# A gated feed-forward and attention kernel: seven-product blocks taken over 288 rows instead of 256

## The chip, the cores and the metric

The kernel runs on one core of one Trainium2 chip. A core has five engines that each run their own list of instructions in order and meet through semaphores: TensorE (PE, matrix products; its weight loads are listed as PEld), VectorE (DVE), ScalarE (ACT), GpSimd (POOL) and SyncE (SP), which here issues all DMA transfers. Matrix products accumulate into PSUM, which has eight banks of 128 partitions by 512 float32. The metric is the time of one execution in microseconds (us), lower is better; a run is compared with others of the same kernel by the median.

## The reference

Input `x` has 2048 positions of 576 values. Two branches work on it and a gate per position mixes them:

```python
g = sigmoid((x * gate_w).sum(-1))
a = A(x)                                   # 32-head attention in 4 segments of 512, with a memory, then @ wo
b = (silu(x @ w_gate) * (x @ w_up)) @ w_down   # 576 -> 4608 -> 576
out = g * a + (1 - g) * b
```

The change touches `x @ w_gate` and `x @ w_up`: 576 rows of the contraction, 4608 output columns each, 2048 positions. All of it is to float32 accuracy, which the kernel gets from a fast product format by splitting each operand into a high part and a low part (what the high part lost) and adding three products: high by high, high by low, low by high.

## The kernel before

The span has a first phase of some 220 us (projections q, k, v of the four segments, and the memory), a second phase to about 1710 us (feed-forward and attention interleaved), and an end (output projection).

**The unit.** The feed-forward is cut into two halves of positions (two segments of 512 each; half 0 is segments 2 and 3, half 1 is segments 0 and 1) and 36 column tiles of 128. A unit is one half and one tile `f`: it makes 128 gate columns and 128 up columns for two blocks of 512 positions. That is a 2 by 2 block product: gate and up stand for the two blocks on one side, the two segments for those on the other, and the contraction is halved. The kernel does it with seven block products instead of eight (a Strassen-Winograd scheme): sums and differences of the blocks are formed ahead, seven products are made, and their results are added up on the way through PSUM. The function `seven` (L934) makes one of them: two 128-row chunks, three terms (high/low) each, so six matmuls over 512 columns. The two halves of the contraction are rows 0 to 255 and 256 to 511. The last 64 rows don't take part: they are held twice in a 128-row operand, and `rest2` (L942) adds them to each of the four outputs with two matmuls, eight a unit.

**The order of a unit** is written out by hand (from L994): product 0 into bank `a`, ACT copies it to bank `xx` (L995); product 1 into bank `y`, ACT copies it to the row `p5` (L998); product 2 onto `a`, DVE adds `a` and `p5` into `y` (L1002); product 3 onto `xx`, copied to `sg0` (L1006); product 4 onto `a`, copied to `xx` (L1010); ACT applies Silu to `sg0` (L1012); product 5 onto `y`, Silu into `sg1` (L1015); the rest onto `a`, DVE adds it to `p5` (L1020); product 6 onto `xx`; DVE multiplies `sg0` by `xx` (L1024) and `sg1` by `p5` (L1025). Product 2 of the next unit goes onto `a` again and so needs the copy L995 of its product 0 to be done; that copy writes `xx`, which L1024 reads.

**Beats.** After each product, and once more after the rest on `a`, the unit calls `tick` (k = 0 to 7). A tick runs what is due at that beat: preparation of coming weights (`defer(o + 1, ...)` of a step with number `o` puts it at k = o of the unit, or at k = o - 8 of the next), splitting of results, groups of the down product (`down_group`, L788) and attention steps. In half 0 every third unit (f divisible by 3, position q = 0) carries sixteen down groups and the attention between its products and lasts some 37 us; the two units after it (q = 1 and q = 2) carry neither and last some 11 us. In half 1 attention goes into all units.

**Weights.** In half 0, `w_make(f)` (L221) makes the operands of the next unit: four sums on POOL (L230), seven high parts on ACT (L234), seven low parts on DVE (L237), and for the last 64 rows two high parts on ACT (L241) and two low parts on DVE (L244); SP stores all of them in DRAM (L247, L250). The raw tiles hold 640 rows' worth (512 and twice 64) and are loaded two units ahead (`w_load`, L202). In half 1 `w_fetch` (L600) loads the stored operands back. Between the halves, ten beats of down groups and attention only let the operands of the second pair of segments be formed (`x_second`, L903). At the end of the first phase the first half's operands of x are formed (`first_sum`, `first_split`), and those steps of unit 0's preparation that have numbers under 8 are worked off by the last eight `v_step` calls, up to three a call; what is left of them runs after the last.

Of the kernel before, what the change touches and what calls it, by code (L numbers as in the profile page):

```python
# [52 lines left out]
SLOT = (0, 3, 2, 1, 4, 6, 5)  # L53
KR = 6 * DH
# [7 lines left out]
def gated_mix(ctx, tc, xT, wf, wd, wv, wo, beta, cmask, ident, bmask, out):  # L62
# [13 lines left out]
    rc = dram.tile([FT, 2, P, 2 * P], F32, name="rc")  # L76
    xsd = dram.tile([2, P, L], F32, name="xsd")
# [63 lines left out]
    def xs_tile():  # L141
        return xo.tile([P, L], F32R, name="xs", bufs=2)

    def x_tiles(s):
        j = 5 * (s % 2)
        return [x_slot(j + kt // 2, kt % 2) for kt in range(4)], xs_tile()
# [52 lines left out]
    def raw_tile():  # L199
        return rp.tile([P, NT * P], F32, name="raw")  # L200

    def w_load(f, u):  # L202
        r = raw_tile().rearrange("p (k n) -> p k n", n=P)
        nc.sync.dma_start(r, wf[f][:, u])
        return r

# [6 lines left out]
    wraw_of, wops, wrem = {}, {}, {}  # L213
# [4 lines left out]
    def rem_tile():  # L218
        return wop.tile([P, 2, P], F32R, name="wr_", bufs=3)

    def w_make(f):  # L221
        g, u = wraw_of.pop(f)
        ops, rem = [None] * 7, [None] * 2
# [25 lines left out]
        def rem_keep(z):  # L249
            nc.sync.dma_start(rc[f, z], f32(rem[z]).rearrange("p a n -> p (a n)"))  # L250
# [16 lines left out]
    with ExitStack() as st:  # L267
        qst_ = ExitStack()
        qps = [pool(qst_, f"qp{i}", 1, side="right") for i in range(2)]
# [13 lines left out]
        raws = {}  # L283

# [213 lines left out]

        FSUM = {4: [(1, 0), (4, 0)], 5: [(2, 0), (1, 1)], 7: [(4, 1), (2, 1)]}
        FSPLIT = {6: [(1, 0), (4, 0)], 7: [(2, 0), (1, 1)], 8: [(4, 1), (2, 1)]}  # L500
        for s in range(NSEG):
            upd = upd_gen(s - 1) if s else None
            casts = []
            for n, (m, u) in enumerate(chains):
# [13 lines left out]
                if (s, n) == (1, 7):  # L518
                    mid.append(betas)
                if s == 3:  # L520
# [13 lines left out]
            if s == 3:  # L534
# [4 lines left out]
                for i in range(NST):  # L539
                    qst.append(kq.tile([P, 2, L], BF, name=f"qst{i}"))  # L540
                    if i < NST - 1:
                        kst.append(kq.tile([P, 2, L], BF, name=f"kst{i}"))
# [5 lines left out]
                wraw_of[0] = [w_load(0, u) for u in range(2)]  # L548
                start = w_make(0)
            for n in range(8):  # L550
# [5 lines left out]
                if s < 2 and n == 6:  # L556
                    late.append((xsd[s], f32(xs_of[s][1])))
# [20 lines left out]
        while start[0][0] < 8:  # L578
            start.pop(0)[1]()
        for z in range(2):  # L580
# [3 lines left out]
    with ExitStack() as st:  # L584
# [15 lines left out]
        def w_fetch(f):  # L600
            ops, rem = [None] * 7, [None] * 2
# [6 lines left out]
            def two(z):  # L608
                rem[z] = rem_tile()
                nc.sync.dma_start(f32(rem[z]).rearrange("p a n -> p (a n)"), rc[f, z])  # L610

            return [(j + 2 if f else FIRST[j], lambda j=j: one(j)) for j in range(7)] + [(4 + 6 * (f == 0) + 4 * z, lambda z=z: two(z)) for z in range(2)]
# [3 lines left out]
        kst.append(kp.tile([P, 2, L], BF, name=f"kst{NST - 1}", bufs=1))  # L616
        defer(8, lambda: nc.gpsimd.memset(kst[NST - 1], -1.0))
# [193 lines left out]
        def c_open():  # L811
# [6 lines left out]
            for n, (hf, kt) in zip((1, 2, 4, 5, 8, 9), ((0, 0), (0, 2), (0, 4), (1, 0), (1, 2), (1, 4))):  # L818
                wo_load(n, hf, slice(kt, min(kt + 2, NT)))
# [3 lines left out]
        def wo_load(n, hf, k):  # L823
# [309 lines left out]
```

## Time and profile before

| what | us |
|---|---|
| median of three runs (lowest, highest) | 1810.26 (1809.39, 1811.24) |
| the profiled execution, time | 1809.34 |
| the profiled execution, span from first to last instruction | 1807.6 |
| PE busy in the span | 1792.1 |
| DVE busy | 1287.7 |
| ACT busy | 960.2 |
| POOL busy | 796.3 |

The span lies 1.7 us under the execution's own time, and that time 0.9 us under the median. Matmuls are pipelined, so a matmul shown as 0.39 us long leaves room for the next one after 0.23 us. A row of the timeline gives the start and the duration in us, the engine, the line of the kernel, the operation, the tiles written and read, shapes and count; in brackets the idle time of the engine before it and what ended that. Consecutive instructions of one engine overlap by about 0.1 us in it, since the next enters while the last drains.

### The profile page before, as it was taken

The page shows a single profiled execution, that of the slowest core. Times are in us where ns is not written, and L with a number is a line of the kernel's source. Part 1 is how long each engine was busy: PE and PEld are TensorE (multiplying, and loading weights), DVE is VectorE, ACT ScalarE, POOL GpSimd, SP SyncE. Part 2 cuts the span into 40 slices and gives each one's busy share as a digit, 9 for nine tenths or more (in the row PEclk, how much of TensorE's full clock was granted, in tenths as well). Part 3 has the DMA queues.
Part 4 walks back from the last instruction along what each step waited for, and adds up shares of the span by engine and source line. Part 5 has one row for each costly group of instructions (what it writes and reads, how often), then busy time and mean ns, then how long its engine had stood idle before and what let it go on. Part 6 is the DMA issues. An engine that isn't in the chain of part 4 may idle for free.

```text
span 1807.6 us, 36471 instructions
## 1 busy us (share of the span) xinstructions
PE 1792.1 (99%) x12517; PEld 1539.4 (85%) x12517; DVE 1287.7 (71%) x3285; ACT 960.2 (53%) x1827; POOL 796.3 (44%) x991
## 2 busy tenths in 40 slices
PE   9999999999999999999989999999999999999999
PEld 7899888888888888888877887887887887888899
DVE  6455666777877787778777677777777777764455
ACT  7656575456655665566546455455455455354511
POOL 3323731344444444444445545555555545553121
PEclk9999999999999999999999999999999999999999
DMA  7444495556746664566467446355455455355544
GB/s 237 161 148 171 152 344 202 163 192 235 239 139 208 238 229 151 194 240 239 134 237 225 147 139 202 124 156 186 141 167 176 136 157 188 117 160 179 195 143 138
DMA packets 204936, 331.34 MB, mean 183 GB/s; under 512 B 38416, under 2 KB 95888, under 8 KB 204752
## 3 DMA queue, kind: packets, MB, share of 16 engines
q1 hardware_dynamic: 204752, 329.02, 54.8%
q8 instruction: 99, 1.62, 0.4%
q14 instruction: 85, 0.70, 0.1%
HBM read 194.33 MB, written 134.61 MB: 182 GB/s over the span
## 4 chain that ended last, share of the span: by engine, by line
PE 94%; DVE 3%; DMA 2%; issue 0%; ACT 0%; SPq 0%; POOL 0%; DVEq 0%; ACTq 0%
PE bank L938 37%; PE bank L798 24%; PE bank L134 12%; PE bank L944 7%; PE bank L674 4%; PE bank L632 4%; PE bank L703 2%; PE bank L705 1%; PE bank L369 1%; DVE xo L112 1%; PE bank L415 1%; DMA kst<-stk 1%; PE bank L857 0%; DMA raw<-in_xT_dram 0%; DVE scr L639 0%
## 5 line engine op out<-in xcount | busy, mean ns | idle before, releaser
L798 PE MATMUL bank<-dw,hh 128*128 128x320 f32 (+1 forms) x2304 | 484.4, 303 | 5.8 <-DVE ya L803 4.9
L768 POOL TENSOR_TENSOR p<-pe,p 128x512 f16<-128x512 f32 x320 | 379.9, 1187 | 175.6 <-DVE p L766 121.0
L798 PEld LDWEIGHTS bank<-dw,hh 128*128 128x128 f32 x2304 | 379.4, 189 | 25.7 <-DVE ya L803 6.4
L678 ACT ACTIVATE pe<-bank 128x512 f32<-128x512 f32 x320 | 190.5, 595 | 330.8 <-PE bank L674 292.7
L798 PE MATMUL bank<-dw,hl 128*128 128x320 f32 (+1 forms) x1152 | 340.2, 295 | 0.3 <-DVE hl L112 0.3
L686 POOL TENSOR_SCALAR_AFFINE_SELECT pe<-pe 128x256 f32<-128x256 f32 (+1 forms) x320 | 144.3, 451 | 325.9 <-ACT pe L678 299.7
L803 DVE TENSOR_TENSOR ya<-bank,ya 128x320 f32<-128x320 f32 x352 | 157.3, 452 | 155.8 <-PE bank L798 151.7
L639 DVE CUSTOM_DVE_ANT_0 scr<-bank,cm 128x512 bf16<-128x512 f32 (+3 forms) x512 | 247.6, 484 | 23.4 <-PE bank L632 15.4
L798 PEld LDWEIGHTS bank<-dw,hl 128*128 128x128 f32 x1152 | 217.6, 189 | 0.9 <-DVE hl L112 0.9
L766 DVE CAST p<-pe 128x512 f16<-128x512 f32 x320 | 155.9, 488 | 0.0
L674 PE MATMUL bank<-qst,kst 111*128 111x512 bf16 (+3 forms) x512 | 150.9, 303 | 0.0
L632 PE MATMUL bank<-kst,qst 108*128 108x512 bf16 (+3 forms) x512 | 126.0, 299 | 2.2 <-DMA kst<-stk 0.9
L882 DVE TENSOR_TENSOR hl<-row,hh 128x512 fp32r<-128x512 f32 x120 | 105.7, 881 | 13.1 <-ACT hh L881 13.1
L1006 ACT ACTIVATE row<-bank 128x512 f32<-128x512 f32 x72 | 43.1, 599 | 122.8 <-PE bank L944 122.7
L230 POOL TENSOR_TENSOR ws<-raw 128x256 f32<-128x256 f32 x72 | 63.5, 882 | 91.7 <-DMA raw<-in_wf_dram 73.5
L1020 DVE TENSOR_TENSOR row<-bank,row 128x512 f32<-128x512 f32 x72 | 49.6, 689 | 70.7 <-PE bank L944 70.7
L1024 DVE TENSOR_TENSOR row<-bank,row 128x512 f32<-128x512 f32 x72 | 49.8, 691 | 58.8 <-PE bank L944 50.4
L134 PE MATMUL bank<-xo,qhi 128*128 128x512 f32 x288 | 91.5, 398 | 0.1
L1010 ACT ACTIVATE bank<-bank 128x512 f32<-128x512 f32 x72 | 41.9, 582 | 82.1 <-PE bank L938 79.7
L325 POOL TENSOR_TENSOR q<-qr,q 128x512 bf16<-128x512 f32 x36 | 43.8, 1216 | 91.9 <-ACT q L324 82.6
L703 PEld LDWEIGHTS <-p 128*128 128x128 f16 x1280 | 69.2, 96 | 10.2 <-issue 6.6
L674 PEld LDWEIGHTS <-kst 111*128 111x128 bf16 x512 | 48.5, 98 | 34.3 <-issue 19.9
(2104 smaller groups left out, 4180.4 us busy)
## 6 DMA issues: line engine op xcount, KB each, us to landing
raw<-in_wf_dram SPq DMA_DIRECT2D x72, 320.0 KB
dc<-dw SPq DMA_DIRECT2D x36, 576.0 KB
dw<-dc SPq DMA_DIRECT2D x36, 576.0 KB
stk<-q SPq DMA_DIRECT2D x32, 384.0 KB
draw<-in_wd_dram SPq DMA_DIRECT2D x36, 288.0 KB
vd<-vps SPq DMA_DIRECT2D x8, 912.0 KB
v<-vd SPq DMA_DIRECT2D x16, 456.0 KB
qst<-stk SPq DMA_DIRECT2D x128, 54.0 KB
```

Of the source, the lines that this page charges most:

```text
L134: nc.tensor.matmul(t, st[n], mv[n], start=(n == 0), stop=(n == 13))
L632: nc.tensor.matmul(t[:, c:c + w], qs[:KR, pr, P * i:P * i + P], ks[:KR, pr, 0:w], start=True, stop=True)
L639: nc.vector.tensor_tensor_reduce(scr[:, :w], t[:, c:c + w], cm[:, L - w:L], 1.0, -3.0e38, OP.add, OP.max, m[:, k:k + 1])
L674: nc.tensor.matmul(t[:, c:c + w], ks[:KR + 3, pr, P * j:P * j + P], qs[:KR + 3, pr, P * j:L], start=True, stop=True)
L678: nc.scalar.activation(pe, t, AF.Exp, scale=SCALE)
L686: nc.gpsimd.affine_select(d, d, pattern=pat, compare_op=OP.is_ge, fill=0.0, base=0, channel_multiplier=-1)
L766: nc.vector.tensor_copy(p1, pe)
L768: nc.gpsimd.tensor_sub(p2, pe, p1)
L798: nc.tensor.matmul(t, p, q[:, cs], start=(n == 0), stop=(n == 3 * CH - 1))
L803: nc.vector.tensor_add(ya[:, i, cs], t, ya[:, i, cs])
L938: nc.tensor.matmul(t, w[:, p, z], x[z][:, q], start=first and n == 0, stop=last and n == 5, skip_group_check=True)
L944: nc.tensor.matmul(t, w[:, p], xs, start=False, stop=p == 1, skip_group_check=True)
```

## The change

The 576 rows are halved as a whole: each block product now goes over 288 rows. Of the last 64 rows the first 32 go with the first half and the other 32 with the second, so they take part in the sums and differences like all others. Their three terms (high by high, high by low, low by high) stand one below the other in one operand of 96 rows, so one more matmul a product covers them: seven matmuls in each of seven products, 49 a unit, where there were 42 and the eight of `rest2`.

- The host hands over two more inputs: the last rows of x and of the two weights, each repeated three times down the partitions.
- `w_make` forms four sums of 96 rows by 128 on POOL (`rem_total`, k = 3, 3, 4, 4), rounds all seven remainder operands at once on ACT (`rem_high`, 96 by 896, k = 5), makes the low part on DVE for rows 64 to 95 (`rem_low`, 32 by 896, k = 6) and stores them with one DMA of 336 KB (`rem_keep`, k = 7). The two ACT copies, two DVE subtractions and two stores of 128 KB for the old rest are gone.
- The raw weight tiles are loaded without the last rows (256 KB instead of 320 KB, twice a unit); `r_load` loads those into a single buffer (192 KB) at k = 7.
- In half 1 one load of 336 KB at k = 1 replaces two of 128 KB.
- The remainder operands of x, seven of 96 by 512, are formed in segments 1 and 2 of the first phase (`rest_load`, `rest_sum`, `rest_split`); those of the second half are stored and fetched back between the halves with seven loads of 192 KB in place of two of 256 KB.
- The DVE addition to `p5` moves from behind the rest on `a` to behind product 4. The two ticks around the removed rest now follow each other with nothing between.
- Two of the four attention buffers `qst` move to another pool, and the output weights are loaded in six pieces by columns.

```diff
-        def rem_high(z, r):
-            rem[z] = rem_tile()
-            nc.scalar.activation(rem[z][:, 0], r, AF.Copy)
-
-        def rem_low(z, r):
-            nc.vector.tensor_sub(rem[z][:, 1], r, f32(rem[z][:, 0]))
+        def rem_total(j):
+            r = rraw_of[f][:RB]
+            o, p, q, sub = {4: (5, 0, 1, True), 1: (1, 1, 3, False), 2: (4, 1, 0, True), 5: (6, 2, 4, True)}[j]
+            (nc.gpsimd.tensor_sub if sub else nc.gpsimd.tensor_add)(r[:, o], r[:, p], r[:, q])
+
+        def rem_high():
+            rem.append(rem_tile())
+            nc.scalar.activation(rem[0][:RB], rraw_of[f][:RB], AF.Copy)
+
+        def rem_low():
+            nc.vector.tensor_sub(rem[0][64:RB], rraw_of.pop(f)[64:RB], f32(rem[0][64:RB]))
...
-        for z, r in ((0, g[:, 4]), (1, u[:, 4])):
-            o = LEAD + 4 + 2 * z
-            todo += [(o, lambda z=z, r=r: rem_high(z, r)), (o + 1, lambda z=z, r=r: rem_low(z, r)),
-                     (o + 2, lambda z=z: rem_keep(z))]
+        todo += [(3 + n // 2, lambda j=j: rem_total(j)) for n, j in enumerate((4, 1, 2, 5))]
+        todo += [(5, rem_high), (6, rem_low), (7, rem_keep)]
...
+    def r_load(f):
+        rraw_of[f] = rp.tile([P, 7, P], F32, name="rr", bufs=1)
+        nc.sync.dma_start(rraw_of[f][:RB, 0:4], wfr[f])
...
+        RSTEP = {4: (0, 3, -1), 5: (5, -4, 1), 6: (-2, 4), 7: (2, -6), 8: (6,)}
...
+                if 1 <= s < 3:
+                    if n == 2:
+                        rest_load(2 - s)
+                    for j in RSTEP.get(n, ()):
+                        mid.append(lambda j=j: rest_split(2 - s, j) if j >= 0 else rest_sum(-j))
...
-            return [(j + 2 if f else FIRST[j], lambda j=j: one(j)) for j in range(7)] + [(4 + 6 * (f == 0) + 4 * z, lambda z=z: two(z)) for z in range(2)]
+            def rest():
+                rem.append(rem_tile())
+                nc.sync.dma_start(f32(rem[0][:RB]).rearrange("p j n -> p (j n)"), rc[f])
+
+            return [(j + 2 if f else FIRST[j], lambda j=j: one(j)) for j in range(7)] + [(1 if f else 10, rest)]
...
-        def seven(t, w, x, first, last):
+        def seven(t, j, first=True):
+            w, x = ops[j], XO[j]
             n = 0
             for z in range(2):
                 for p, q in ((0, 0), (0, 1), (1, 0)):
-                    nc.tensor.matmul(t, w[:, p, z], x[z][:, q], start=first and n == 0, stop=last and n == 5,
+                    nc.tensor.matmul(t, w[:, p, z], x[z][:, q], start=first and n == 0, stop=False,
                                      skip_group_check=True)
                     n += 1
+            nc.tensor.matmul(t, rem[:RB, RPOS[j]], XR[j][:RB], start=False, stop=True, skip_group_check=True)
 
-        def rest2(t, w, xs):
-            for p in range(2):
-                nc.tensor.matmul(t, w[:, p], xs, start=False, stop=p == 1, skip_group_check=True)
...
                 if half == 0 and f + 2 < FT:
+                    plan.append((7, lambda f=f: r_load(f + 2)))
...
-            seven(a, w[4], XO[4], False, True)
+            seven(a, 4, False)
             xx = x_tile()
             nc.scalar.activation(xx, a, AF.Copy)
+            nc.vector.tensor_add(p5, a, p5)
             tick()
             nc.scalar.activation(sg0, sg0, AF.Silu)
-            seven(y, w[5], XO[5], False, False)
-            rest2(y, wr[0], XS[1])
+            seven(y, 5, False)
             nc.scalar.activation(sg1, y, AF.Silu)
             if half or q == 0:
                 exp_table()
             tick()
-            rest2(a, wr[1], XS[1])
-            nc.vector.tensor_add(p5, a, p5)
             tick()
-            seven(xx, w[6], XO[6], False, False)
-            rest2(xx, wr[1], XS[0])
+            seven(xx, 6, False)
             nc.vector.tensor_mul(sg0, xx, sg0)
             nc.vector.tensor_mul(sg1, p5, sg1)
```

More of the change, by code (lines that the diff above doesn't have):

```diff
@@ L579, in gated_mix @@
             start.pop(0)[1]()
+        r_load(1)
         for z in range(2):
@@ L616, in gated_mix @@
         kst.append(kp.tile([P, 2, L], BF, name=f"kst{NST - 1}", bufs=1))
+        for i in range(2, NST):
+            qst.append(kp.tile([P, 2, L], BF, name=f"qst{i}", bufs=1))
         defer(8, lambda: nc.gpsimd.memset(kst[NST - 1], -1.0))
```

113 lines of the change are left out of this document (67 added, 46 removed).

## The prediction, made before the result was known

> **What bounds the kernel now.** I read the page first (busy times, chain of work that ended last), then the waits of PE, then the chain in order of time for the pitch of a matmul.
>
> ```profile
> span 1807.6 us, 36471 instructions
> ...
> PE 1792.1 (99%) x12517; PEld 1539.4 (85%) x12517; DVE 1287.7 (71%) x3285; ACT 960.2 (53%) x1827; POOL 796.3 (44%) x991
> ...
> PE 94%; DVE 3%; DMA 2%; issue 0%; ACT 0%; SPq 0%; POOL 0%; DVEq 0%; ACTq 0%
> PE bank L938 37%; PE bank L798 24%; PE bank L134 12%; PE bank L944 7%; PE bank L674 4%; PE bank L632 4%; PE bank L703 2%; PE bank L705 1%; PE bank L369 1%; DVE xo L112 1%; PE bank L415 1%; DMA kst<-stk 1%; PE bank L857 0%; DMA raw<-in_xT_dram 0%; DVE scr L639 0%
> ```
> ```profile
> PE bank L798 <- DVE ya L803: 4.9, 6, 1.7
> ```
> ```profile
> 227.92 2.72 PE bank L938 x12
> 230.64 0.91 PE bank L944 x4
> ```
>
> PE is busy for 99% of the span and carries 94% of the chain; its largest wait sums to 4.9 us. So PE's issue is the time, and whatever makes PE wait is added to it in full. Twelve matmuls of the products take 2.72 us and four of the rest 0.91: 0.227 us each. The profiled execution took 1809.34 us (span 1807.6), 0.9 under the median of 1810.26; I sum changes and add them to either.
>
> **Matmuls removed.** A unit goes from 42 + 8 = 50 to 49 matmuls, in 72 units: 72 x 0.227 = 16.3 us less on PE. The new ones have 96 rows. The trace has no such row count; nearest are 111 rows:
>
> ```profile
> L134 PE MATMUL bank<-xo,qhi 128*128 128x512 f32 x288 | 91.5, 398 | 0.1
> ...
> L674 PE MATMUL bank<-qst,kst 111*128 111x512 bf16 x128 | 50.0, 391 | 0.0
> ```
>
> 398 ns with 128 rows, 391 with 111: the rows cost nothing and save nothing, and I take 0.227 for the new ones too. Half of the 16.3, 8.2 us, falls in half 1, where the operands are only fetched (80 KB more a unit, on SP, off PE's path) and nothing else is added: I count it in full.
>
> **What half 0 adds, and where.** Only units q = 1 and q = 2 (and unit 0, which has no down groups yet) are tight, as the stretches of one group of three show; the third row is from the first phase.
>
> ```profile
> 467.86:479.38 11.52, 11.52 (x54) 9.52 (x52) 9.77 (x20) 8.88 (x18) 6.97 (x9) 1.00 0.59 191
> 479.38:490.71 11.33, 11.33 (x51) 9.38 (x50) 9.37 (x17) 8.58 (x22) 3.01 (x5) 1.00 1.02 372
> ...
> 50.00:100.00 50.00, 50.00 (x298) 44.87 (x297) 26.90 (x73) 32.65 (x66) 17.00 (x19) 1.00 0.43 146
> ```
>
> The columns after the length are PE, PEld, DVE, ACT, POOL, clock, DMA share, GB/s. By busy time there is room: DVE 9.4 of 11.3, ACT 8.6. But these engines work in order, so I follow the order at the end of unit q = 1 (start 467.86), with these prices for the two new operations, whose size of 896 elements a partition lies beside 870:
>
> ```profile
> L111 ACT ACTIVATE vw<-xo 128x870 fp32r<-128x870 f32 x1 | 0.9, 917 | 0.0
> ...
> L112 DVE TENSOR_TENSOR vw<-xo,vw 128x870 fp32r<-128x870 f32 x1 | 1.1, 1066 | 0.7 <-ACT vw L111 0.7
> ```
> ```profile
> 475.30 1.52 PE L938 MATMUL bank<-xo,wo__5755 128*128 128x512 f32 x6
> 476.66 0.61 PE L944 MATMUL bank<-xs,wr__5655 128*128 128x512 f32 x2
> 477.11 0.62 PE L944 MATMUL bank<-xs,wr__5772 128*128 128x512 f32 x2
> 477.56 1.52 PE L938 MATMUL bank<-xo,wo__5769 128*128 128x512 f32 x6
> ...
> 479.38 1.52 PE L938 MATMUL bank<-xo,wo__5810 128*128 128x512 f32 x6
> ...
> 482.10 1.52 PE L938 MATMUL bank<-xo,wo__5837 128*128 128x512 f32 x6
> ```
> ```profile
> 477.77 0.63 ACT L1012 ACTIVATE row<-row 128x512 f32<-128x512 f32 x1
> 478.31 0.58 ACT L1015 ACTIVATE row<-bank 128x512 f32<-128x512 f32 x1
> 478.79 0.41 ACT L234 ACTIVATE wo__5837<-ws 128x256 fp32r<-128x256 f32 x1
> 479.10 0.41 ACT L234 ACTIVATE wo__5846<-raw 128x256 fp32r<-128x256 f32 x1
> ...
> 480.94 0.58 ACT L995 ACTIVATE bank<-bank 128x512 f32<-128x512 f32 x1 [0.35 <-DVE row L1025]
> ```
> ```profile
> 479.65 0.69 DVE L1024 TENSOR_TENSOR row<-bank,row 128x512 f32<-128x512 f32 x1 [0.86 <-PE bank L944]
> 480.26 0.68 DVE L1025 TENSOR_TENSOR row<-row 128x512 f32<-128x512 f32 x1
> ```
> ```profile
>   ACT bank L995: 9.4, 17
> ```
>
> I take 0.95 us for `rem_high` and 1.10 for `rem_low`, by elements per partition; that the latter spans 32 partitions and not 128 might make it as short as a quarter, 0.27, which is the lower end used below.
>
> Take product 5's start, 475.30, as 0. Before: product 6 runs from 2.26 to 4.08; DVE multiplies at 4.35 (L1024) and 4.96 (L1025); the copy L995 starts when L1025 ends, at 5.64 (the last row: it waited for L1025 17 times), ends at 6.22, and product 2 of the next unit, which needs it, is due at 6.80. Slack 0.58.
>
> After: PE needs 4 products of 7 matmuls up to that product 2, so it is due at 28 x 0.227 = 6.35. ACT is unchanged up to the high part at 3.49 (478.79, k = 5), since the Silu table holds it up and not PE. Behind that high part, at 3.80, now stands `rem_high`, 0.95 long, to 4.75. `rem_low` is DVE's next at k = 6, right after, because the second tick has no PE work in front of it any more; it waits for `rem_high`, starts at 4.78 and lets DVE go on 1.02 later (1.10 less the 0.08 by which neighbours overlap), at 5.80. L1024 and L1025 are queued behind it: 5.80 and 6.41, end 7.09. L995 runs 7.09 to 7.67, and product 2 starts at 7.72, not 6.35: **PE waits 1.37 us**. Twelve q = 1 units do this: 16.4 us.
>
> At the end of q = 2 no table load stands ahead, and a split of `dw` stands between:
>
> ```profile
> 486.63 1.52 PE L938 MATMUL bank<-xo,wo__5885 128*128 128x512 f32 x6
> ...
> 488.64 0.60 ACT L1015 ACTIVATE row<-bank 128x512 f32<-128x512 f32 x1 [0.33 <-PE bank L944]
> ...
> 490.15 0.76 DVE L882 TENSOR_TENSOR dw<-draw,dw 128x576 fp32r<-128x576 f32 x1
> ```
>
> From product 5's start 486.63: Silu (L1015) 0.20 behind the eight matmuls (1.81) before, so at 1.79 after seven (1.59); high part 0.50 later at 2.29, `rem_high` 2.60 to 3.55, `rem_low` 3.58, DVE free at 4.60, `dw` to 5.30, L1024, L1025 to 6.59, L995 to 7.17, product 2 at 7.22 instead of 6.35: 0.87 us. Eleven q = 2 units make weights for a next one: 9.6 us. In q = 0 units with down groups three groups of 9 matmuls lie between k = 5 and k = 6: nothing.
>
> Unit 0 has no groups, and the reload of the exponential's table stands ahead of its high part:
>
> ```profile
> 232.13 0.58 ACT L1015 ACTIVATE row<-bank 128x512 f32<-128x512 f32 x1
> ...
> 234.13 0.40 ACT L234 ACTIVATE wo__2641<-ws 128x256 fp32r<-128x256 f32 x1
> ```
>
> 2.00 us from L1015 to it, not 0.48 as in q = 1: the wait is 1.37 + 1.52 = 2.9 us, once.
>
> **The start of unit 0.** Of its preparation 21 steps instead of 15 have numbers under 8, and 17 fit into the `v_step` calls. In order, `rem_high` falls to the seventh call and `rem_low` to the eighth, behind that call's DVE work:
>
> ```profile
> 220.74 1.63 PE L938 MATMUL bank<-xo,wo__2349 128*128 128x512 f32 x6
> ...
> 224.21 0.46 DVE L422 TENSOR_TENSOR q<-bank,dn 128x288 f32<-128x288 f32 x1
> ...
> 226.26 1.20 PE L938 MATMUL bank<-xo,wo__2434 128*128 128x512 f32 x4 [0.21 <-DVE wo__2434 L237]
> ```
>
> Product 0's seventh matmul, due at 220.74 + 1.36 = 222.10, now needs `rem_low`, which ends at 224.67 + 1.10 = 225.8: 3.7 us. Before, the 21st matmul came at 226.26 and not at 220.74 + 20 x 0.227 = 225.28, so 1.0 was lost there already. Net 2.7.
>
> **The rest, at nothing.** Phase one: seven copies of 0.6 us on ACT, seven DVE subtractions of 0.7, four POOL sums of 1.2 a segment, under PE's full 50 us where ACT has 32.65 and DVE 26.90; if a transpose's copy comes late behind two of them, 1 us a segment at most. Between the halves 832 KB more are loaded, 2.3 us at the 372 GB/s above if exposed; needed only after the down groups, and loaded behind what waits there now. DVE's earlier addition to `p5` runs where DVE waits for PE. POOL's four sums (each between nothing and the 0.73 of a 128x256 one) come 9 us ahead of need in q = 1. In q = 2 they need `r_load`, which stands on SP behind `rem_keep`, and so behind `rem_low`:
>
> ```profile
> 478.42 1.09 SPq L204 DMA_DIRECT2D raw<-in_wf_dram  x1
> ...
> 484.18 0.73 POOL L230 TENSOR_TENSOR ws<-raw 128x256 f32<-128x256 f32 x1 [4.51 <-DMA raw<-in_wf_dram]
> ```
>
> A load issued in that dense stretch (DMA share 1.02) is used 5.8 us later. `rem_low` of q = 1 ends at 5.9, the load goes out at 6.4, lands at 12.2, the sums are done by 14.1 (0.46 each); `rem_high` of q = 2 is due at 12.5 + 2.6 = 15.1. One us of slack; I take nothing, and a microsecond or two per group of three as the upper end.
>
> **Sum.** -16.3 + 16.4 + 9.6 + 2.9 + 2.7 = +15.3 us: 1824.6 for an execution like the profiled one, 1825.6 as a median.
>
> **The rivals.** *Hidden, faster (other side).* The remainder chain stays off PE's path, as the idle fifth of DVE and ACT suggests; only the start's 2.7 remains: 1810.26 - 16.3 + 2.7 = 1796.7. Place: L995 at the head of units q = 2 and q = 0. It decides if `rem_high` and `rem_low` together cost 0.6 us instead of 1.97, or if L1024 doesn't queue behind `rem_low`. The order of the code speaks against it. Chance 0.13.
>
> *The copy released one step earlier.* L995 needs only L1024's result; if it waits no longer for L1025, each of 24 waits is 0.61 shorter: 1825.6 - 14.6 = 1811.0, no change. Against it: the 17 waits above. 0.04.
>
> *POOL slows DVE.*
>
> ```profile
> L882 DVE TENSOR_TENSOR hl<-row,hh x120: 676/686/1424, 237.8 to 1717.3; 128x512 fp32r<-128x512 f32 x120
> ```
>
> One subtraction of two SBUF operands takes 0.68 or up to 1.42 us. If POOL's sums (late by a late `r_load`, or t4 and t5 of the same beats) lie over `rem_low`, it takes twice as long: 24 x 1.0 more, 1850. Against it: POOL is busy for 3.0 of 11.3 us in q = 2. 0.08. The Trainium skill says the same of the engines (GPSIMD Engine Reference, "Key points": the SBUF interfaces are shared, and GpSimd contends with DVE instructions of two SBUF inputs); the trace agrees with its 1.42 beside 0.68.
>
> *A removed matmul is worth its weight load too.*
>
> ```profile
> L798 PEld LDWEIGHTS bank<-dw,hh 128*128 128x128 f32 x2304 | 379.4, 189 | 25.7 <-DVE ya L803 6.4
> ```
>
> If loads did not lie under running matmuls, each removed pair were worth 0.227 and its load, 0.189 by a row of equal shape, 0.416 in all: 72 x 0.416 = 30.0, 13.7 more than I count, so 1811.9, no change. Twelve pairs in 2.72 us exclude it nearly: 0.01. The Trainium skill states it (TensorE: Matmul & The Clock Gate, "The mechanism": loads overlap running matmuls only where the row groups differ); the trace disagrees, with 0.227 for a pair in equal row groups.
>
> **How the numbers follow.** Forecast 0.74, rivals 0.13, 0.04, 0.08, 0.01. About 0.2% (3.6 us) is what a measurement of this kernel tells from no change. Faster: 0.13. Within: 0.05. Slower: 0.74 + 0.08 = 0.82. The likeliest case's own range is 1814 to 1837 (0.4 us either way on 24 waits, and the start). With `rem_low` at 0.27 each wait is 0.8 shorter (0.57, 0.07, 2.1, start 1.9): -16.3 + 6.8 + 0.8 + 2.1 + 1.9 = -4.7, or 1805.6. So the range is 1806 to 1846: it takes in that end, the two no-change cases and half of the slowed DVE, and leaves out the hidden case.
>
> **What would show it.** PE idle ahead of product 2 (the third product's first matmul) by some 1.4 us in each q = 2 unit and 0.9 in each q = 0 unit of half 0, put down to the ACT copy behind product 0; DVE idle on `rem_high` ahead of a 1.1 us subtraction; half 1 shorter by 8 us and half 0 longer by some 23, its start included; 3.7 us of wait at the seventh matmul of unit 0. If half 0 shows no such wait, the forecast is wrong in its main step; if the waits are there with other lengths, `rem_low` or L1025's release is mis-sized.

## The result, and the profile after

The changed kernel takes 1859.88 us (median of 4 runs, 1859.72 to 1862.87); the kernel before, beside it, 1810.75. The ratio is 1.0274, with a 95% interval of 1.0256 to 1.0292. The forecast was 1825.6 with a range of 1806 to 1846: the direction was right, the size was not, +49 us in place of +15.3. The profiled execution took 1862.87, the longest of the four; its profile lies about 3 us above the others, which is why the profiled spans below differ by 53.6 us and the medians by 49.1.

The page of the changed kernel, its busy times and its chain:

```profile
span 1861.2 us, 36473 instructions
...
PE 1805.4 (97%) x12445; PEld 1530.7 (82%) x12445; DVE 1318.9 (71%) x3263; ACT 981.1 (53%) x1805; POOL 891.0 (48%) x1143
...
PE 81%; DVE 6%; ACT 5%; DMA 3%; issue 3%; SPq 1%; POOL 0%; ACTq 0%; DVEq 0%; POOLq 0%
```

PE carried 94% of the chain before and carries 81% now; DVE and ACT have come in. The waits of PE, largest first (total, times, longest):

```profile
PE bank L983 <- DVE rh L251: 19.4, 14, 3.7
PE bank L839 <- DVE ya L844: 18.5, 15, 2.1
PE bank L673 <- ACT pe L719: 3.6, 10, 0.4
```

In the changed file L980 is a product's six matmuls, L983 its 96-row matmul, L248 `rem_high`, L251 `rem_low`, L839 the down groups' matmul, L844 DVE's addition behind it, L673 an attention matmul and L719 the attention's exponential. The sum of DVE's L844 stood at 4.9 before; the other two are new. One group of three units before (only its last row is new here) and after, then the two halves of each; the columns are those of the prediction's stretches:

```profile
550.79:588.07 37.28, 37.28 (x309) 33.12 (x308) 29.49 (x82) 17.55 (x35) 17.29 (x23) 1.00 0.50 167
...
220.74:941.28 720.54, 713.47 (x4655) 616.64 (x4654) 565.40 (x1361) 410.84 (x854) 298.64 (x369) 1.00 0.61 211
941.28:1807.64 866.36, 860.01 (x6583) 728.84 (x6581) 594.58 (x1622) 409.81 (x698) 407.33 (x516) 1.00 0.52 163
```
```profile
557.08:568.51 11.43, 11.43 (x52) 9.37 (x51) 9.41 (x18) 7.85 (x15) 9.41 (x13) 1.00 0.50 152
568.51:581.21 12.70, 11.56 (x50) 9.16 (x49) 8.96 (x15) 9.24 (x20) 6.45 (x9) 1.00 1.00 357
581.21:620.89 39.68, 37.98 (x308) 32.93 (x307) 32.06 (x82) 18.89 (x36) 19.01 (x26) 1.00 0.50 168
...
221.94:995.26 773.32, 729.76 (x4618) 613.89 (x4617) 594.47 (x1328) 426.47 (x819) 386.43 (x510) 0.99 0.61 204
995.26:1861.16 865.90, 856.59 (x6547) 722.98 (x6545) 585.61 (x1622) 409.10 (x698) 401.77 (x516) 1.00 0.54 166
```

All of the loss is in half 0: 720.5 to 773.3 us. Half 1, forecast 8.2 us shorter, is 0.5 shorter. In half 0 the q = 1 unit is level, the q = 2 unit is 1.4 us longer, and the long q = 0 unit, in which I had expected nothing but a wait at its head, is 2.4 us longer. Adding up the units' lengths (start to start of a unit's first matmul) tells where the 53.6 us of the profiled spans come from:

| part | before | after | difference | forecast |
|---|---|---|---|---|
| up to unit 0 | 220.74 | 221.94 | +1.2 | 0 |
| units 0 to 2 | 35.32 | 45.26 | +9.9 | +6.3 |
| q = 0, 11 units (3 to 33) | 403.97 | 431.29 | +27.3 | +7.1 |
| q = 1, 11 units (4 to 34) | 126.66 | 126.77 | +0.1 | -2.5 |
| q = 2, 10 units (5 to 32) | 113.33 | 126.60 | +13.3 | +11.4 |
| unit 35 and the break | 41.26 | 43.41 | +2.2 | +1.1 |
| half 1 | 866.36 | 865.89 | -0.5 | -8.2 |

The head of a q = 2 unit in the trace after, in order of time:

```profile
568.51 1.54 PE L980 MATMUL bank<-xo,wo__6748 128*128 128x512 f32 x6
...
569.08 0.94 ACT L248 ACTIVATE rh<-rr 96x896 fp32r<-96x896 f32 x1
...
570.05 1.08 DVE L251 TENSOR_TENSOR rh<-rr,rh 32x896 fp32r<-32x896 f32 x1 [2.09 <-ACT rh L248]
...
571.17 0.69 DVE L1059 TENSOR_TENSOR row<-bank,row 128x512 f32<-128x512 f32 x1
...
571.20 0.50 PE L983 MATMUL bank<-xr,rh 96*128 96x512 f32 x1 [1.14 <-DVE rh L251]
...
571.78 0.68 DVE L1060 TENSOR_TENSOR row<-row 128x512 f32<-128x512 f32 x1
571.96 0.58 ACT L1034 ACTIVATE bank<-bank 128x512 f32<-128x512 f32 x1 [0.75 <-DVE row L1059]
```

The two durations were forecast at 0.95 and 1.10 and are 0.94 and 1.08; `rem_low` indeed stands on DVE ahead of the multiplications of the unit before, and waits for ACT. But PE doesn't stop at product 2, for the copy. It stops at the seventh matmul of product 0, which reads `rem_low`'s own result. The copy itself (L1034) starts at 571.96, when the first of the two multiplications has ended (571.86), and doesn't wait for the second (572.46).

In the q = 0 unit the same instruction hits something else:

```profile
610.56 1.94 DVE L251 TENSOR_TENSOR rh<-rr,rh 32x896 fp32r<-32x896 f32 x1
612.53 0.49 DVE L844 TENSOR_TENSOR ya<-bank,ya 128x320 f32<-128x320 f32 x1
...
613.08 0.41 PE L839 MATMUL bank<-dw,hh 128*128 128x320 f32 x1 [1.34 <-DVE ya L844]
```

Here `rem_low` takes 1.94 us, beside attention work on POOL (all 25 that run while POOL is idle take 1.08; of the 11 beside POOL's work 10 take 1.93 to 1.94):

```profile
610.35 1.21 POOL L809 TENSOR_TENSOR p<-pe,p 128x512 f16<-128x512 f32 x1 [1.12 <-PE bank L715]
611.51 1.26 POOL L727 TENSOR_SCALAR_AFFINE_SELECT pe<-pe 128x256 f32<-128x256 f32 x1
```

The addition that empties the accumulator of a down group waits behind it, and the next down group has nowhere to write.

### The profile page after: what moved, and what is told of

Its sections match the earlier page's. It is cut to its first block, busy times and chain, and to the rows that moved or that the text cites. A ratio compares the mean times of both kernels' runs of the same rounds, so it can differ in the third digit from the quotient of the medians.

```text
span 1861.2 us, 36473 instructions
## 1 busy us (share of the span) xinstructions
PE 1805.4 (97%) x12445; PEld 1530.7 (82%) x12445; DVE 1318.9 (71%) x3263; ACT 981.1 (53%) x1805; POOL 891.0 (48%) x1143
## 4 chain that ended last, share of the span: by engine, by line
PE 81%; DVE 6%; ACT 5%; DMA 3%; issue 3%; SPq 1%; POOL 0%; ACTq 0%; DVEq 0%; POOLq 0%
PE bank L980 32%; PE bank L839 21%; PE bank L136 11%; PE bank L983 6%; PE bank L715 3%; PE bank L673 3%; DVE rh L251 2%; PE bank L744 2%; ACT rh L248 1%; PE bank L746 1%; ACT L1051 1%; SPq L781 1%; DVE xo L114 1%; DMA kst<-stk 1%; PE bank L379 1%
## 5 line engine op out<-in xcount | busy, mean ns | idle before, releaser
L839 PE MATMUL bank<-dw,hh 128*128 128x320 f32 (+1 forms) x2304 | 489.7, 305 | 21.2 <-DVE ya L844 18.5
L839 PEld LDWEIGHTS bank<-dw,hh 128*128 128x128 f32 x2304 | 379.5, 190 | 41.6 <-DVE ya L844 21.9
L719 ACT ACTIVATE pe<-bank 128x512 f32<-128x512 f32 x320 | 190.0, 594 | 320.1 <-PE bank L715 297.6
L839 PE MATMUL bank<-dw,hl 128*128 128x320 f32 (+1 forms) x1152 | 341.1, 296 | 0.3 <-DVE hl L114 0.3
L844 DVE TENSOR_TENSOR ya<-bank,ya 128x320 f32<-128x320 f32 x352 | 157.6, 454 | 116.1 <-PE bank L839 111.5
L983 PE MATMUL bank<-xr,rh 96*128 96x512 f32 x504 | 202.8, 402 | 19.4 <-DVE rh L251 19.4
L839 PEld LDWEIGHTS bank<-dw,hl 128*128 128x128 f32 x1152 | 218.0, 189 | 0.9 <-DVE hl L114 0.9
L715 PE MATMUL bank<-qst,kst 111*128 111x512 bf16 (+3 forms) x512 | 152.2, 305 | 0.0
L807 DVE CAST p<-pe 128x512 f16<-128x512 f32 x320 | 149.1, 466 | 0.0
L983 PEld LDWEIGHTS bank<-xr,rh 96*128 96x128 f32 x504 | 94.9, 188 | 49.4 <-DVE rh L251 25.4
L673 PE MATMUL bank<-kst,qst 108*128 108x512 bf16 (+3 forms) x512 | 126.5, 300 | 6.9 <-ACT pe L719 3.6
L1049 DVE TENSOR_TENSOR row<-bank,row 128x512 f32<-128x512 f32 x72 | 49.7, 690 | 77.8 <-ACT bank L1048 77.7
L244 POOL TENSOR_TENSOR rr<-rr 96x128 f32<-96x128 f32 x144 | 82.0, 570 | 10.3 <-DMA rr<-in_wfr_dram 2.6
```

The lines of the kernel that those rows point to most:

```text
L673: nc.tensor.matmul(t[:, c:c + w], qs[:KR, pr, P * i:P * i + P], ks[:KR, pr, 0:w], start=True, stop=True)
L715: nc.tensor.matmul(t[:, c:c + w], ks[:KR + 3, pr, P * j:P * j + P], qs[:KR + 3, pr, P * j:L], start=True, stop=True)
L719: nc.scalar.activation(pe, t, AF.Exp, scale=SCALE)
L807: nc.vector.tensor_copy(p1, pe)
L839: nc.tensor.matmul(t, p, q[:, cs], start=(n == 0), stop=(n == 3 * CH - 1))
L844: nc.vector.tensor_add(ya[:, i, cs], t, ya[:, i, cs])
```

## The experiments

**Preparation earlier.** In the order of the steps alone: the sums at beat 0, the high part at 2, the low part at 3, the store and the next load at 4, and the same at the start of unit 0.

```diff
-        todo += [(3 + n // 2, lambda j=j: rem_total(j)) for n, j in enumerate((4, 1, 2, 5))]
-        todo += [(5, rem_high), (6, rem_low), (7, rem_keep)]
+        todo += [(0, lambda j=j: rem_total(j)) for j in (4, 1, 2, 5)]
+        todo += [(2, rem_high), (3, rem_low), (4, rem_keep)]
...
-                    plan.append((7, lambda f=f: r_load(f + 2)))
+                    plan.append((4, lambda f=f: r_load(f + 2)))
```

> The changed kernel with the remainder steps of a unit moved ahead: the four sums at k = 0, rem_high at k = 2, rem_low at k = 3, rem_keep and r_load at k = 4, and as many steps of unit 0's preparation run in the first phase as have numbers under 8. Theory 'place' (rem_low stands at k = 6 behind rem_high at k = 5, blocks DVE and comes too late for the seventh matmul of the next unit's product 0): the waits of that matmul go, a group of three units of half 0 falls from 63.8 us to about 60, units 0 to 2 by some 9 us, the whole from 1860 to about 1811. Rival 'load' (the 192 KB load r_load comes late in the dense units): it is also loaded with more room here, so the same. Rival 'amount' (the added work on ACT, DVE and POOL is too much wherever it stands): stays above 1845.

1830.4 us, ratio 1.0108 (1.0092 to 1.0125): 29.5 of the 49 us are gone with no operation removed, so the place of the preparation in the order is what costs them. The q = 0 units sum to 401.6 us, below the 403.97 of before, and PE's waits on `rem_low` are gone. But 1811 was not reached. Of the 21.4 us by which this span is still longer than the one before, 11.3 lie in the q = 2 units, where a new wait came; 4.9 lie ahead of unit 3, 3.9 in unit 35 and the break, 3.1 in the q = 1 units. The new wait (first two lines: waits of PE; then the trace of the second longest):

```profile
PE bank L981 <- ACT bank L1049: 7.6, 8, 2.3
PE bank L840 <- DVE ya L845: 2.6, 4, 1.1
```
```profile
609.41 0.87 SPq L207 DMA_DIRECT2D rr<-in_wfr_dram  x1
...
615.73 2.36 POOL L244 TENSOR_TENSOR rr<-rr 96x128 f32<-96x128 f32 x4 [5.64 <-DMA rr<-in_wfr_dram]
618.12 0.95 ACT L248 ACTIVATE rh<-rr 96x896 fp32r<-96x896 f32 x1 [2.75 <-POOL rr L244]
...
619.76 0.58 ACT L1049 ACTIVATE bank<-bank 128x512 f32<-128x512 f32 x1
...
620.39 0.96 PE L981 MATMUL bank<-xo,wo__7703 128*128 128x512 f32 x3 [1.90 <-ACT bank L1049]
```

The load issued at 609.41 lets POOL go 6.3 us later (4.9 to 7.0 in the ten q = 2 units); POOL holds ACT's high part, and that holds the copy (L1049) that product 6 needs. (The same lines of the file stand a few lower in some of these kernels.)

**128 rows.** The fourth set of 32 rows is filled: the weights' with another copy, x's with zeros that DVE makes.

```diff
-RB = 96
+RB = 128
...
+            nc.vector.tensor_sub(XR[j][96:128], raw[96:128], raw[96:128])
```

> The changed kernel with the remainder operands widened from 96 to 128 rows (the last 32 rows of the x operand are zero), all else in its place. Theory 'rows' (a matmul of 96 rows among those of 128 costs about 26 ns more a product): the mean pitch in products falls from 231.6 to 227 ns, half 1 by 6 to 7 us, the whole by 12 to 13, to about 1847. Rival 'none' (the pitch has another cause, the operand's place or the accumulation): no change, within 3 us of 1860.

1864.16 us, ratio 1.0293 (1.0277 to 1.0308): no gain, though the matmuls did become faster. In the chain, in order of time, at the start of a q = 1 unit, the changed kernel and this one:

```profile
559.01 1.37 PE bank L980 x6
560.38 0.23 PE bank L983
560.61 1.38 PE bank L980 x6
561.99 0.23 PE bank L983
562.22 1.38 PE bank L980 x6
```
```profile
567.62 1.37 PE bank L981 x6
568.99 0.23 PE bank L984
569.22 1.36 PE bank L981 x6
570.58 0.23 PE bank L984
570.80 1.36 PE bank L981 x6
```

From product to product 1.60 to 1.61 us become 1.58 to 1.60. In single starts: from each 96-row matmul on the distances are 232, 238, 232 and 231 ns before 227 comes back, some 25 ns more than four times 227. That is so in every second q = 1 unit, this one among them; in the others they are 242, 237, 240, 235, 233 and 236, some 60 ns more in all, and why is not shown. With 128 rows nearly all stay at 226 to 227. Over all distances under 300 ns between successive matmuls of products (1400 to 1500 a half; units 3 to 34, and half 1) the means are 227.7 and 229.3 ns before, 231.5 and 231.0 after, and 228.5 and 229.4 with 128 rows. The total doesn't show it, for two reasons. Unit 0 begins at 233.64, 11.7 us later, behind the seven added subtractions a segment (in a kernel further below, with the zeros from outside, it begins at 222.85); and the q = 0 and q = 2 units are as long as they were (39.65 and 12.63 for 39.68 and 12.70), because there DVE sets the time: PE's wait at the seventh matmul grew from 1.14 to 1.22. Half 1, where no such wait stands, fell by 3.3 us (865.9 to 862.6), half of the 6 to 7 expected.

**No low part.** `rem_low` is left out, so the third term of the last 64 rows is missing; the rest is as it was.

```diff
-            nc.vector.tensor_sub(rem[0][64:RB], rraw_of.pop(f)[64:RB], f32(rem[0][64:RB]))
+            rraw_of.pop(f)
```

> The changed kernel without rem_low: the low part of the weight remainder isn't formed, so the third term of the last 64 rows is left out (its rows hold the high part again). Theory 'place', DVE's part: the seventh matmul of product 0 then waits for rem_high alone, 0.2 us instead of 1.3, and in q = 0 units DVE's additions to ya come in time (1.5 us less); ACT's delay of 0.6 stays. A group of three falls from 63.8 to about 61, the whole to about 1832. If ACT alone is the cause, less than 10 us go.

1820.86 us in one run: 39 of the 49 us hang on this one instruction, 36 times, at its place; that is 11 us more than the theory gave it. PE's waits after:

```profile
PE bank L839 <- DVE ya L844: 4.5, 6, 1.2
PE bank L673 <- ACT pe L719: 3.6, 10, 0.4
PE bank L980 <- ACT bank L1034: 2.3, 12, 0.3
```

L844 is back near the 4.9 of before. The q = 0 units still take 38.1 us for 37.3. By successive starts 0.54 of that stands at the attention's matmuls, for an exponential that is queued behind the high part at beat 5, and some 0.2 is a wait for the copy L1034 ahead of product 2; the rest is the pitch.

**No reload.** The 192 KB of rows are loaded once and used for all 36 blocks; the other 35 loads are left out.

```diff
     def r_load(f):
+        if f:
+            rraw_of[f] = rr0[0]
+            return
         rraw_of[f] = rp.tile([P, 7, P], F32, name="rr", bufs=1)
+        rr0.append(rraw_of[f])
```

> The changed kernel with r_load done once: all units form their remainder from the tile of unit 0, so the 192 KB load of the other 35 units is left out and never waited for. Theory 'place': no change, 1855 to 1862, since the sums on POOL are done before rem_high is due. Rival 'load': the waits go and the whole falls below 1840.

1858.95 us in one run. The late load is no cause in the changed kernel, as the prediction took it; it becomes one only when the preparation is moved ahead, as in the first experiment.

**96 rows in the kernel before.** The eight rest matmuls of the old unit run over 96 of their 128 rows; part of those products is left out.

```diff
-                nc.tensor.matmul(t, w[:, p], xs, start=False, stop=p == 1, skip_group_check=True)
+                nc.tensor.matmul(t, w[:96, p], xs[:96], start=False, stop=p == 1, skip_group_check=True)
```

> The kernel before, with the eight matmuls a unit on the last 64 rows run over 96 of their 128 rows (the last 32 rows of both operands are left out, so part of those products is missing); nothing else changes, no wait of another engine is touched. Theory 'rows' (a matmul of 96 rows between matmuls of 128 rows costs TensorE about 26 ns a switch pair, as the successive starts of 232, 238, 232 and 231 ns round each 96-row matmul of the changed kernel suggest): the eight matmuls stand in four to five places a unit, so 72 units x 3 to 4 places x 26 ns = 5.6 to 7.5 us more, 1816 to 1818. Rival (the longer pitch comes from something else in the changed kernel): no change, 1809 to 1812.

1817.54 us, ratio 1.0038 (1.0024 to 1.0051): +6.7, inside the 5.6 to 7.5 of the theory. The work is less and no wait is touched, and the mean distances rise to 230.1 and 230.7 ns. So a 96-row matmul among 128-row ones is dearer, not equally dear, and this cost needs nothing else of the change. It comes to 23 to 31 ns for each of the 3 to 4 places a unit, though two or four 96-row matmuls stand in a place and one in the changed kernel; that speaks for the change of the row count, and not the rows by themselves, as what costs.

**The load later in the q = 2 unit, and 128 rows with zeros from outside.** Two kernels on top of the first experiment. In the q = 2 units the sums go to beat 3, high and low part to 4 and 5, the store and the next load to 6; the second also has rows 96 to 127, with x's zeros passed in, so that no engine makes them.

```diff
+        b = 3 if f % CH == 0 and f else 0
...
+        todo += [(4, rem_high), (5, rem_low), (6, rem_keep)] if b else [(2, rem_high), (3, rem_low), (4, rem_keep)]
```

> As e1_early, but in the unit with q=2 the sums stand at step 3, the high part at 4, the low part at 5, the store at 6 and the next load at 6, since there the load issued one unit earlier lands only 6.3 us after its issue (609.41 to 615.73 in e1_early's trace) and held POOL, then ACT, then the copy ahead of product 6. Theory 'late load': the waits of product 6 on that copy (0.3 to 2.3 us in each of the eleven q=2 units, about 8 us in all) go, 1820 to 1824. Rival (the work itself, not the load, is too much for these units): 1828 to 1833.

> As e7_byunit, with the rest matmul over 128 rows, where rows 96 to 127 of its x operand are zeros passed in with x and those of the weights a fourth copy; 64 KB more to load, store and fetch a unit. Theory 'rows': pitch in products back from 231.6 to 228.5 ns in half 0 and from 231.2 to 229.8 in half 1, 36 x 49 x 3.1 + 36 x 49 x 1.4 ns = 8 us less than e7_byunit, 1812 to 1816. Rival (TensorE is not what paces the units, as in e2_rows128 where the time did not fall): the same as e7_byunit within 2 us, or more where the added bytes delay the loads.

1835.05 us, ratio 1.0130 (1.0114 to 1.0147): a miss. The waits of the q = 2 units went (11.4 us each), and came back at the head of the q = 0 units: up to 1.3 on the copy L1036 and up to 0.9 on the low part. Moving the steps doesn't make the load earlier. The second kernel: 1825.18, ratio 1.0076 (1.0063 to 1.0090), 9.9 us less. PE still waits 15.0 us in sum for the copy L1036, but for the low part only 1.8 us, where the 128-row kernel above waits 20.9; so PE sets more of the time and the rows count.

**A queue of its own, or an earlier load.** Three kernels on top of the first experiment. One issues the load from ACT. The second issues it at the first beat of the unit before, for which a second tile was needed; to find its room, the sums moved to a tile of their own (so high and low part are two instructions each) and the exponentials of the attention have three tiles, not four. The third is the second with 128 rows.

```diff
-        nc.sync.dma_start(rraw_of[f][:RB, 0:4], wfr[f])
+        (nc.scalar if f > 1 else nc.sync).dma_start(rraw_of[f][:RB, 0:4], wfr[f])
```
```diff
-        rraw_of[f] = rp.tile([P, 7, P], F32, name="rr", bufs=1)
+        rraw_of[f] = [(fp if f and f % 2 == 0 else rp).tile([P, 4, P], F32, name="rr", bufs=1)]
...
-                    plan.append((4, lambda f=f: r_load(f + 2)))
+                    plan.append((0, lambda f=f: r_load(f + 2)))
```

> As e1_early, with the load of the last 64 rows of the weights issued from ScalarE's own queue, not from SyncE's, at the same step. In e7_byunit the wait for that load only moved from product 6 of the q=2 unit to the first products of the q=0 unit (1.3 us on the copy, up to 1.0 on the low part), so the load is what is late, 6.3 us behind its issue in the stretch where the transfers fill the 16 engines (share 1.0). Theory 'behind the others' (it stands in SyncE's queue behind two 256 KB loads of the other rows): from a queue of its own it lands earlier, and some of the 0.3 to 2.3 us in the q=2 units goes, 1822 to 1828. Rival (the 16 engines are full, whichever queue asks): 1829 to 1832; a ScalarE that waits with its issue could cost more, up to 1840.

> As e1_early, but two tiles for the loaded rows, so that the load is issued at the first step of the unit before, some 7 to 9 us sooner; to make room the three sums have a tile of their own (the high and the low part become two instructions each) and the attention's exponentials have three tiles, not four. Theory 'late load': the waits of product 6 in the q=2 units, about 8 us in all in e1_early, go: 1820 to 1825. Rival (the load is not the cause, or two instructions in place of one cost more than the wait): 1829 to 1836.

> As e10_load2, with the rest matmul over 128 rows, rows 96 to 127 of its x operand being zeros passed in with x. Theory 'rows': 8 to 10 us less than e10_load2 (e8_byunit128 stood 9.9 below e7_byunit), 1811 to 1815: then every loss that was found but the break between the halves is undone and the kernel is level with the one before. Rival: the added 64 KB a unit make the loads late again, and less than 5 us is won.

The own queue gives 1828.7 us, ratio 1.0104 (1.0088 to 1.0121): level with the first experiment and above the 1822 to 1828 of the theory. The wait on L1049 is all but gone (0.3 us, once), but the load is only some 0.5 us earlier: from its issue to POOL's first sum the ten q = 2 units now show 4.4 to 6.3 us, in the median 4.5 for 5.1. These units sum to 121.5 us for 124.6, but the q = 0 units to 406.5 for 401.6. ACT now waits for its turn to issue:

```profile
609.81 1.28 ACT L1052 ACT_TABLE_LOAD   x1 [2.03 <-DVE rh L251]
...
621.54 0.36 ACTq L207 DMA_DIRECT2D rr<-in_wfr_dram  x1
621.95 0.63 ACT L1052 ACTIVATE row<-row 128x512 f32<-128x512 f32 x1 [1.52 <-DVE rh L251]
```

The tile is free only when `rem_low` has read it, and in those 1.5 to 2 us ACT's Silu can't run. Whether that is what the q = 0 units lose was not tried. The earlier load gives 1821.46, ratio 1.0070 (1.0052 to 1.0089), 9 us below the first experiment: POOL no longer waits for it at all. With 128 rows it is 1811.44, ratio 1.0008 (0.9998 to 1.0018), level with the kernel before. Its group of three units:

```profile
591.32:602.91 11.59, 11.45 (x52) 9.14 (x50) 10.08 (x19) 9.04 (x17) 9.40 (x12) 1.00 0.58 195
602.91:614.15 11.24, 11.24 (x50) 9.31 (x50) 10.91 (x18) 9.11 (x22) 6.32 (x9) 1.00 1.01 362
614.15:651.12 36.97, 36.97 (x308) 32.99 (x307) 31.45 (x82) 18.29 (x36) 19.98 (x27) 1.00 0.50 181
```

59.80 us, where the kernel before has 60.13. Three matmuls fewer should have given 0.68. About 0.3 of it is lost at the end of the q = 1 unit: the next unit's first matmul starts 0.3 us late, when DVE's addition to `p5` (L1055) has emptied bank `a`, and that addition is queued behind the low part, now two instructions. Nine q = 1 units show this wait.

**Another order at the start.** On top of the last kernel: block 0's rows have a tile of their own, its sums, high and low part come two to three steps later, and block 1's rows are loaded earlier in the first phase.

```diff
+        todo += [(0 if f else 2 + n // 2, lambda j=j: rem_total(j)) for n, j in enumerate((4, 1, 2, 5))]
+        todo += [(2, rem_high), (3, rem_low), (4, rem_keep)] if f else [(5, rem_high), (6, rem_low), (8, rem_keep)]
```

> As e11_load2_128, with another order in the first segment's end alone: the loaded rows of block 0 get a tile of their own, and the sums, the high and the low part of block 0 come two to three steps later, so that ScalarE does not stand 1.9 us at 214.8 for a sum of POOL that is queued behind POOL's own work (DVE then stood 4.3 us, and unit 0 began at 223.15, 2.4 us later than in the kernel before, and was 14.3 us long, not 12.5). Theory 'order at the start': unit 0 begins at 221 to 222 and the total falls by 1.5 to 3.5 us, to 1808 to 1810. Rival (the added operations fill that stretch whatever their order): no change, 1811 to 1812; or a new wait at product 0's seventh matmul, up to 1814.

1810.02 us, ratio 0.9999 (0.9990 to 1.0008). Unit 0 begins at 221.57, 1.6 us sooner, as the theory had it, and the total is 1.4 lower, just short of the 1.5 to 3.5 expected and no more than the spread of the runs. It is the best version found, and it is level with the kernel before, not ahead of it.

## Why the prediction was wrong

Two steps failed above all. The q = 0 units were put at "nothing" because PE has other work there, without asking what stands on DVE and ACT behind the new instructions; that line of the table is 20.2 us above its forecast, of 38.3 us in all. And a matmul of 96 rows was priced like one of 128. A third step, the place of the q = 1 wait, was wrong too, and the size came out near all the same.

**The matmuls: -16.3 forecast.** The count was right, the price was not. That "the rows cost nothing and save nothing" was read from two kinds of matmul that don't alternate with others; alternation is what costs, as far as the runs tell. With 128 rows in place of 96 the same program got 9.9 and 10.0 us shorter (1835.05 to 1825.18, 1821.46 to 1811.44). So some 10 of the 16.3 are taken back by the rows alone, where PE's other waits don't hide it.

**q = 1 into q = 2: +1.37 forecast, 1.3 measured, at another place.** The durations and `rem_low`'s place in DVE's queue were as told. The step that failed is "PE needs 4 products of 7 matmuls up to that product 2": I followed the copy, and overlooked that product 0 itself ends in a matmul that reads the low part. I had used just this for unit 0. `rem_low` ends at 571.13, the seventh matmul is due at 569.90 (568.51 + 1.39) and starts at 571.20, 1.3 late (the profile counts 1.14 of it as idle). The path of the copy was wrong by itself as well: the copy starts 0.1 us after the first multiplication (571.86 to 571.96), 0.5 before the second ends. That is the rival *The copy released one step earlier*, given 0.04: in the changed kernel it is so at the head of every q = 2 unit of half 0, though in the kernel before the copy started when the second one ended. On that path alone the wait would have been 0.61 shorter, 0.76. That the size agrees is luck.

**q = 0: "nothing", the largest error.** I counted 0.87 at its head and nothing inside, since three groups of nine matmuls lie between the beats. They lie on PE; the question was who waits on DVE and ACT. Measured: 27.3 us over 11 units where the table has 7.1, so 1.84 us a unit more. PE stands 1.3 us at a down group, for the additions queued behind a `rem_low` of 1.94, and 0.4 at an attention matmul, for an exponential behind `rem_high`. By successive starts (units 9 to 33) a unit's down groups grew by 1.70, its attention by 0.53, its products and rest by 0.25 though a matmul fewer. The runs without the low part (38.1 a unit) and with both parts early (37.1) show the cause: the place in the two queues. The 0.87 at the head itself was not there (0.1).

**POOL slows DVE: chance 0.08, and true in q = 0.** Not the sums of the change slowed `rem_low`, as that rival said, but attention work that was there already; 1.08 us at the head of q = 2, 1.94 in q = 0, with the counts given above.

**Unit 0 and 1: +5.6 forecast with the start.** The first wait was forecast at 3.7 and is 3.66; the second, forecast at 2.9 ahead of product 2, is 2.55 and stands at the seventh matmul. Not foreseen is what comes behind them:

```profile
227.23 0.76 PE L983 MATMUL bank<-xr,rh 96*128 96x512 f32 x1 [3.66 <-DVE rh L251]
...
227.79 2.69 PE L980 MATMUL bank<-xo,wo__2460 128*128 128x512 f32 x6
```
```profile
223.00:226.00 3.00, 0.57 (x3) 0.14 (x1) 2.28 (x7) 2.14 (x6) 1.40 (x2) 1.00 0.46 166
226.20:229.60 3.40, 2.37 (x6) 1.92 (x7) 3.37 (x6) 0.90 (x2) 1.06 (x1) 0.60 1.01 391
```

The granted clock (the column before the DMA share) is 0.60 on average in the stretch after the wait: the trace has one half from 226.85 to 230.27. Matmuls follow each other at 427 ns there, not 227, up to eight times: 8 x 0.2 = 1.6 us at most behind each of the two waits. Both together, some 3 us, are most of the 3.6 by which this line of the table was missed. Two more stretches at half clock, at 356.56 and 970.96, fall into the lines of q = 0 and of unit 35 and the break.

**Half 1: -8.2 forecast, -0.5 measured.** Successive starts in half 1, added up by the line of the first: the rest matmuls fell from 67.1 to 59.6 us, as 36 matmuls fewer should give; but the block products rose from 365.4 to 366.8, the down groups from 238.6 to 240.9 and the distances that begin at an attention matmul of L715 (L674 before) from 42.4 to 45.8. The first rise is the 96 rows: in the kernel of 1811.44, with 128, products and rest read 365.0 and 58.3, 9.2 us less than before. Still that half is only 1.3 us shorter than before, since the down groups (241.1) and L715's distances (45.6) stay dear there. Of the last rise, 2.4 us are idle time of PE behind these matmuls; the profile puts waits of L673 (2.8 in sum, 1.3 before) and of L980 (1.2, none before) down to transfers. Whether the added loads made these transfers late was not tried, and why the down groups got dearer stays open.

**The rest at nothing.** The late load cost nothing that the run without reloads could show (1858.95 for 1859.88), as forecast. The first phase cost 1.2 us, within the 1 us a segment that I gave as its upper end.

## What to carry to other kernels

When an operation is put into the queue of an engine that works in order, list for each kind of stage what stands behind it there and who waits for that, and list every reader of its result, the first one above all; a stage in which the bound engine has plenty of other work is not covered if that work itself passes through the queue. The same instruction cost 39 us at beat 6, and at beat 3 no wait of PE on its result was left. And a matmul on fewer rows among full ones is not cheaper: fill the rows.

## What the runs showed of the hardware

A 96-row matmul between 128-row ones costs about 25 ns beside its own 227, spread over the four distances from its start on (232, 238, 232 and 231 ns), in half of the q = 1 units and some 60 in the other half; in all 6.7 us in the kernel before, and 9.9 and 10.0 us in two versions of the changed one, 20 ns for each of its 504. The Trainium skill (TensorE: Matmul & The Clock Gate, "Step-by-step: what each phase is for") says of the weight load that the row count doesn't matter. The trace agrees for the load itself (188 ns with 96 rows, 189 with 128); the change of the row count from one matmul to the next does matter here.

The granted clock falls to one half for 3.413 us at a time. In the changed kernel these stretches begin at 226.85, 243.92, 356.56 and 970.96 us, which is 5, 38 and 218 times 3.413 after the first; PE's idle time in the 3.413 us before each was 3.3, 2.4, 2.1 and 1.9 us. In the traces of all thirteen kernels, each cut into pieces of 3.413 us on its own such grid, PE's idle time taken by the profile's ends of matmuls, half clock followed on each of the 16 pieces with 1.85 us or more of idle time, on two of six with 1.6 to 1.75, and on one below that, at the start of a span. So no single wait's length decides, but idle time of about half a piece: matmuls at 427 ns came behind a wait of 1.70 us in the run with 96 rows in the kernel before, and did not behind one of 1.7 in the run without a low part. The Trainium skill (the same page, "What's actually happening") gives 1.2 GHz after an idle window of about 3.4 us and calls the window free-running. The trace agrees with the length of the window and with its free running; that the whole window be idle was not needed here.

A DVE subtraction of 896 elements on 32 partitions takes 1.08 us, as long as one of 870 on 128 partitions (1.07): partitions left out save nothing. Beside POOL's work it takes up to 1.94.
